# Parameter loads on ScalarE's queue, an activation load ahead of the C matrices, and a negated sine table on VectorE, in a fused S5 + SwiGLU kernel

## The chip, the cores and the metric

The kernel runs on one core of a Trainium2 chip. The metric is the device time of one execution in microseconds, taken as the median over several runs. Beside the runs there is one profiled execution, whose trace is what the views below are read from. All times inside the trace count from the first instruction of the span.

## What is computed

The input `x` (2048 rows of 512 numbers, bf16) is normalised row by row, and three terms are added: the input itself, a state-space layer (S5) and a gated feed-forward layer, both fed by the normalised rows.

```python
xn = layernorm(x)
# S5: diagonal complex recurrence over the 2048 rows
dt      = exp(log_dt);  Lam_bar = exp(dt * (Lambda_re + 1j*Lambda_im))
B_bar   = ((Lam_bar - 1) / Lam)[:, None] * (B_re + 1j*B_im)
Bu      = xn @ B_bar.T
h[t]    = Lam_bar * h[t-1] + Bu[t]
ya      = 2 * (h @ (C_re + 1j*C_im).T).real + xn * Dskip
# SwiGLU, 1376 hidden columns
yb      = (silu(xn @ w_gate) * (xn @ w_up)) @ w_down
out     = x + ya + yb
```

## The kernel before, in words

**Tiling.** The 2048 rows are handled in four chunks of 512 rows (16 tiles of 128 rows). The tile `x_sb` holds all of x, `xn_sb` normalised rows, `xnT` (two buffers, chunk number modulo 2) their transpose, which TensorE (PE) multiplies with the weights. For each chunk PE computes the gate columns (`wg`, line 742) and the up columns (`wu`, line 742) in groups of two 128-column tiles, the leftover columns of two chunks at once (`ffn_left`, lines 820 and 830), the product with B (`BT`, line 857), and at the end the down projection (`wd` with `hT`, line 940, called dA below) and the product with C (`W12` with `hss`, line 953, called dB). dA and dB add up in the same PSUM bank.

**PSUM.** The eight banks are used as four pairs in turn. A group of PE writes a pair, ScalarE (ACT) reads it out (silu into `sg` at line 754, gate; copy into `uf` at line 810, up; copy into `u_sb` at line 864, B; lines 839 to 844, leftover), and only then may the fourth group after it write the same pair.

**Recurrence.** Turning the complex recurrence by a running phase makes it real: VectorE (DVE) multiplies with a cosine table `cosT` and a sine table `sin2` (both tables hold 512 steps for each of four groups of 128 states), scans (line 897), and multiplies back (line 888). `sin2` holds the sine and, beside it, the negated sine. The tables are made in `_tables`: ACT forms the angle (`tm`, line 689), DVE reduces it to one period (lines 691, 693 for sine, 699, 701 for cosine, `scrC`), and ACT applies Sin (lines 695, 697, 703). The small per-state numbers (`sm`, lines 613 to 663, 634, 632) come from three parameter vectors that are loaded as rows of `prow` and transposed by PE (line 565) into `praw`.

**Layer norm.** Chunk 0 is normalised tile by tile in halves at the start, so that PE can begin early (lines 509 to 530 on DVE, `sd` at line 521 on ACT, transposes by PE at line 568). Chunks 1 to 3 take statistics on DVE (lines 479, 483), variance plus epsilon and the power on GpSimd (POOL, lines 487, 491). Chunk 1 is then normalised by DVE (line 495); chunks 2 and 3 by ACT (line 503) after DVE has made `nmr`, minus mean over deviation (line 500). The transpose of chunks 1 to 3 into `xnT` is a DMA transpose (`xt_chunk_dma`, named xTd1 to xTd3 here).

**Order.** Every step is a task of a graph. PE and SyncE (SP) execute their tasks in the order in which the program adds them. For ACT, DVE and POOL `_schedule` chooses the order when the program is built: it keeps a clock per engine from the `est` of each task and, for a DMA, from a byte count, and picks by longest remaining path. So an `est` that is altered costs nothing itself but can reorder ACT and DVE. Each DMA waits in SP's own queue for what it depends on; a DMA transpose waits for every DMA that was added before it, and every later DMA waits for the last transpose:

```python
if xpose:
    after = after + tuple(dma_tasks)
...
else:
    if xp_state[0] is not None:
        after = after + (xp_state[0],)
```

So from `x4` on the loads go one after the other in program order: B_re, B_im (transposes), xTd1, C_re, C_im (transposes), then `ld_x8` (rows of chunk 2), `ld_wd0`, `ld_wd1`, `ld_x12`, `ld_dsk`, then xTd2. On ACT's queue three DMAs stand before any arithmetic: `ld_touch`, a read of 64 short pieces of the gate weights into a tile `tch` that nothing uses, and two parts of the gate weights, `a0` and `a1` (the third, `a2`, is on SP).

Of the kernel before, what the change touches and what calls it, by code (L numbers as in the profile page):

```python
# [10 lines left out]
ALU = alu_op_type.AluOpType  # L11
F32 = mybir.dt.float32
B16 = mybir.dt.bfloat16
I32 = mybir.dt.int32
AF = mybir.ActivationFunctionType

_DBG = {}
_CFG = dict(
    ln_norm_act=(False, False, True, True),
    prio_tab=0.0,  # L20
    prio_par=0.0,
    prio_xt=4000.0,
)
MAGIC = 12582912.0
TWO_PI = 2.0 * math.pi
# [224 lines left out]
def bass_parallel_sum__ssm_conv_s5__swiglu_ffn__prompt_kernel(  # L250
# [23 lines left out]
    KT = D // 128  # L274
# [6 lines left out]
    g = _Graph()  # L281
    es = ExitStack()
    with es:
        block = es.enter_context(nc.Block(no_gpsimd_drain=True))

        def sb(name, shape, dt):
            return es.enter_context(nc.sbuf_tensor(name, shape, dt))
# [7 lines left out]
        x_sb = sb("x_sb", [128, NT, D], B16)  # L295
# [11 lines left out]
        sin2 = sb("sin2", [128, PT, 2, TP], B16)  # L307
# [11 lines left out]
        tz = scrC[:, 2048:3072].rearrange("p (b t) -> p b t", b=2)  # L319
# [4 lines left out]
        mv = sb("mv", [128, NT, 2], F32)  # L324
        ve = sb("ve", [128, NT], F32)
        rstd = sb("rstd", [128, NT], F32)
        nmr = sb("nmr", [128, NT], F32)
        mhalf = sb("mhalf", [128, NT], F32)
        st0 = sb("st0", [128, 4, 2, 6], F32)
        sd0 = sb("sd0", [128, 4], F32)  # L330
        epst = sb("epst", [128, 1], F32)
        tch = sb("tch", [16, KT, 2], B16)
        praw = sb("praw", [128, 3, PT], B16)
        prow = sb("prow", [12, 128], B16)
        ecst = sb("ecst", [128, PT], F32)
# [1 line left out]
        NSM = 64  # L337
        sm = sb("sm", [128, NSM, PT], F32)
# [44 lines left out]
        x_v = A_x[0].rearrange("(a p) d -> p a d", p=128)  # L383
        out_v = out[0].rearrange("(a p) d -> p a d", p=128)
        wg_v = B_w_gate.rearrange("(k p) f -> p k f", p=128)
# [5 lines left out]
        def dma(name, dst, src, writes, nbytes, reads=(), after=(), out_=False, eng="sp", xpose=False, prio=0.0, order=(), **kw):  # L391
            after = tuple(after)
            if xpose:
                after = after + tuple(dma_tasks)
                fn = lambda e, dst=dst, src=src: e.dma_start_transpose(out=dst, in_=src)
                est, nb = 2000.0, int(nbytes * 1.2)
            else:
                if xp_state[0] is not None:
                    after = after + (xp_state[0],)
                fn = lambda e, dst=dst, src=src: e.dma_start(dst, src, **kw)  # L400
                est, nb = 330.0 + nbytes / 900.0, nbytes
            t = g.add(eng, fn, reads=reads, writes=writes, name=name, dma=True, after=after, out=out_, est=est, nbytes=nb, prio=prio, order=order)
            dma_tasks.append(t)
            if xpose:
                xp_state[0] = t
            return t

        TILEB = 128 * D * 2
# [4 lines left out]
        def pload(name, slot, src, **kw):  # L413
            return dma(name, prow[4 * slot:4 * slot + 4, :], src.rearrange("(a p) -> a p", p=128), [("prow", slot)], 1024, **kw)

        def x_load(a, **kw):
            return dma("ld_x%d" % a, x_sb[:, a:a + 1, :], x_v[:, a:a + 1, :], [("x", a)], TILEB, **kw)

        def wg_load(nm, k0, k1, **kw):
            return dma("ld_wg" + nm, wg[:, k0:k1, 0:FG], wg_v[:, k0:k1, 0:FG], [("wg", nm)], (k1 - k0) * 128 * FG * 2, **kw)  # L420

        x_load(0)
        x_load(1)
        act_q = [dma("ld_touch", tch[0:16], wg_v[0:128:8, :, 0:2], [("tch",)], 16 * 16, eng="act")]
        act_q.append(wg_load("a0", 0, 2, eng="act", order=(act_q[-1],)))
        x_load(2)
        act_q.append(wg_load("a1", 2, 3, eng="act", order=(act_q[-1],)))
        wg_load("a2", 3, 4)
        x_load(3)
        pload("ld_ldt", 2, A_log_dt)  # L430
        pload("ld_lim", 1, A_Lambda_im)
        pload("ld_lre", 0, A_Lambda_re)
        dma("ld_wu0", wu[:, :, 0:FH0], wu_v[:, :, 0:FH0], [("wu", 0)], 512 * FH0 * 2)
        dma("ld_wg1", wg[:, :, FG:Fh], wg_v[:, :, FG:Fh], [("wg", 1)], 512 * (Fh - FG) * 2)
# [5 lines left out]
            dma("ld_bim", BT[:, 1], A_B_im, [("BT", 1, kt) for kt in range(KT)], 512 * 512 * 2, xpose=True)  # L440

        def loads_stage_b2():
            dma("ld_cre", CT[:, 0], A_C_re, [("CT", 0)], 512 * 512 * 2, xpose=True)
            dma("ld_cim", CT[:, 1], A_C_im, [("CT", 1)], 512 * 512 * 2, xpose=True)
            dma("ld_x8", x_sb[:, 8:12, :], x_v[:, 8:12, :], [("x", a) for a in range(8, 12)], 4 * TILEB)
            dma("ld_wd0", wd[:, 0:FT - 1, :], B_w_down[0:(FT - 1) * 128, :].rearrange("(k p) d -> p k d", p=128), [("wd", 0)], (FT - 1) * 128 * 1024)
            dma("ld_wd1", wd[0:fsz[-1], FT - 1, :], B_w_down[(FT - 1) * 128:Fh, :], [("wd", 1)], fsz[-1] * 1024)
            dma("ld_x12", x_sb[:, 12:16, :], x_v[:, 12:16, :], [("x", a) for a in range(12, 16)], 4 * TILEB)
            dma("ld_dsk", dsk[:], A_Dskip.partition_broadcast(128), [("dsk",)], 128 * 1024)
# [6 lines left out]
              reads=[("ones",)], writes=[("ident",)], name="ident", est=300)  # L456
        g.add("pool", lambda e: e.iota(iot[:], pattern=[[1, TP]], base=0, channel_multiplier=0, allow_small_or_imprecise_dtypes=True),
              writes=[("iot",)], name="iota", est=1000)
# [1 line left out]
        g.add("pool", lambda e: e.memset(car[:, 0], 0.0), writes=[("car", 0, 0), ("car", 0, 1)], name="car0", est=100)  # L460
        g.add("pool", lambda e: e.memset(ecst[:], math.e), writes=[("ecst",)], name="ecst", est=100)
        def act_table(func, order):
            g.add("act", lambda e: e.activation(out=sm[:, NSM - 1, 0:1], in_=epst[:], func=func, bias=epst[:, 0:1]), reads=[("epst",)], writes=[("sm", "_warm")],
                  name="act_warm", est=1500, order=order)

        act_table(AF.Sqrt, (act_q[-1],))
# [18 lines left out]

        def ln_ve(a, n, eng="dve", order=()):
            return g.add(eng, lambda e: e.tensor_scalar(out=ve[:, a:a + n], in0=mv[:, a:a + n, 1], scalar1=EPS, scalar2=None, op0=ALU.add),
                         reads=[("mv", a + j) for j in range(n)], writes=[("ve", a + j) for j in range(n)], name="ve%d" % a, est=70 if eng == "dve" else 230, order=order)

        def ln_rstd(a, n):  # L490
            return g.add("pool", lambda e: e.tensor_tensor(out=rstd[:, a:a + n], in0=ve[:, a:a + n], in1=mhalf[:, a:a + n], op=ALU.pow),
                         reads=[("ve", a + j) for j in range(n)] + [("mhalf",)], writes=[("rstd", a + j) for j in range(n)], name="rstd%d" % a, est=370 + 190 * n)

        def ln_apply(a, order=()):
            return g.add("dve", lambda e: e.tensor_scalar(out=xn_sb[:, a % NXN, :], in0=x_sb[:, a, :], scalar1=mv[:, a, 0:1], scalar2=rstd[:, a:a + 1],
# [103 lines left out]
        def S(name):  # L599
            if name not in SMI:  # L600
                SMI[name] = len(SMI)
                assert len(SMI) <= NSM
            return sm[:, SMI[name], :]
# [81 lines left out]
        def _tables():  # L685
            thn = S("thn")
            for pt in range(PT):
                b = pt % 2
                g.add("act", lambda e, pt=pt, b=b: e.activation(out=tm[:, b, :], in_=iot[:], func=AF.Identity, scale=thn[:, pt:pt + 1]),
                      reads=R("thn") + [("iot",)], writes=[("tm", b)], name="tm%d" % pt, est=620, prio=_CFG['prio_tab'], order=(hold["evac"],))  # L690
                g.add("dve", lambda e, b=b: e.tensor_scalar(out=tt1[:, b, :], in0=tm[:, b, :], scalar1=MAGIC, scalar2=None, op0=ALU.add),
                      reads=[("tm", b)], writes=[("tt1", b)], name="tt1s%d" % pt, est=400, prio=_CFG['prio_tab'])
                g.add("dve", lambda e, b=b: e.scalar_tensor_tensor(out=tz[:, b, :], in0=tt1[:, b, :], scalar=MAGIC, in1=tm[:, b, :], op0=ALU.subtract, op1=ALU.subtract),
                      reads=[("tt1", b), ("tm", b)], writes=[("tz", b)], name="tzs%d" % pt, est=660, prio=_CFG['prio_tab'])
                g.add("act", lambda e, pt=pt, b=b: e.activation(out=sin2[:, pt, 0, :], in_=tz[:, b, :], func=AF.Sin, scale=-TWO_PI),
                      reads=[("tz", b)], writes=[("sinT", pt, 0)], name="sinT%d" % pt, est=620, prio=_CFG['prio_tab'])
                g.add("act", lambda e, pt=pt, b=b: e.activation(out=sin2[:, pt, 1, :], in_=tz[:, b, :], func=AF.Sin, scale=TWO_PI),
                      reads=[("tz", b)], writes=[("sinT", pt, 1)], name="msinT%d" % pt, est=620, prio=_CFG['prio_tab'])
                g.add("dve", lambda e, b=b: e.tensor_scalar(out=tt1[:, b, :], in0=tm[:, b, :], scalar1=0.25, scalar2=MAGIC, op0=ALU.add, op1=ALU.add),
                      reads=[("tm", b)], writes=[("tt1", b)], name="tt1c%d" % pt, est=400, prio=_CFG['prio_tab'])  # L700
                g.add("dve", lambda e, b=b: e.scalar_tensor_tensor(out=tz[:, b, :], in0=tt1[:, b, :], scalar=MAGIC, in1=tm[:, b, :], op0=ALU.subtract, op1=ALU.subtract),
                      reads=[("tt1", b), ("tm", b)], writes=[("tz", b)], name="tzc%d" % pt, est=660, prio=_CFG['prio_tab'])
                g.add("act", lambda e, pt=pt, b=b: e.activation(out=cosT[:, pt, :], in_=tz[:, b, :], func=AF.Sin, scale=-TWO_PI, bias=halfpi[:, 0:1]),  # L703
                      reads=[("tz", b), ("halfpi",)], writes=[("cosT", pt)], name="cosT%d" % pt, est=700, prio=_CFG['prio_tab'])
# [367 lines left out]
```

## Time and profile before

| | us |
|---|---|
| median of 6 runs | 180.72 (179.88 to 181.54) |
| the profiled execution | 181.39 |
| its span, first to last instruction | 179.6 |
| PE busy in the span | 174.1 (97%) |
| DVE busy | 162.3 (90%) |
| ACT busy | 88.9 (49%) |
| POOL busy | 9.8 (5%) |

The time of the profiled execution holds 1.79 us that lie around the span. Matmuls are pipelined, so a row of PE shows as busy also while one matmul waits for the one in front of it; an idle PE is the surer sign. "Idle before" names what an engine waited for; a wait for several things is put down to the one that came last. The granted TensorE clock is 1.000 for the whole span.

### The profile page before, as it was taken

The numbers are of one execution on the slowest core, as the hardware profiler recorded it, in microseconds if no ns is written. First come the engines' busy times: TensorE is split into PE (matmuls) and PEld (weight loads), VectorE is DVE, ScalarE is ACT, GpSimd is POOL, SyncE is SP. The second block draws the span as 40 slices with busy tenths as digits, with TensorE's granted clock in tenths as the row PEclk, the third lists the DMA queues.
The fourth block names the chain that finished last, engine by engine and source line by source line (L and its number), as shares of the span: only waits on it lengthen the run. The fifth ranks groups of instructions, "written<-read, shape, count | busy, mean of one in ns | idle before, by whom it ended". The sixth has DMA issues, their size and how long they took to land.

```text
span 179.6 us, 2421 instructions
## 1 busy us (share of the span) xinstructions
PE 174.1 (97%) x929; PEld 83.9 (47%) x937; DVE 162.3 (90%) x281; ACT 88.9 (49%) x114; POOL 9.8 (5%) x21
## 2 busy tenths in 40 slices
PE   8899999999979999999999999999999999999994
PEld 2694444444424444444444444444444444444743
DVE  2958984886799999999999999999999999999983
ACT  4469999999499976106656552000965620000000
POOL 3013300000500000040000000000000000000000
DMA  5995585569551000002340000001100000000122
GB/s 166 376 323 96 111 88 95 111 130 362 174 98 22 0 0 0 0 0 65 83 91 0 0 0 4 0 0 58 58 0 4 0 0 0 0 0 4 58 83 92
DMA packets 22978, 12.37 MB, mean 69 GB/s; under 512 B 15192, under 2 KB 22968, under 8 KB 22968
## 3 DMA queue, kind: packets, MB, share of 16 engines
q1 hardware_dynamic: 22472, 11.54, 25.2%
q10 hardware_dynamic: 496, 0.69, 1.1%
q8 instruction: 7, 0.11, 0.3%
q14 instruction: 3, 0.02, 0.1%
HBM read 6.46 MB, written 2.10 MB: 48 GB/s over the span
## 4 chain that ended last, share of the span: by engine, by line
PE 93%; DMA 2%; ACT 2%; DVE 1%; issue 0%; SPq 0%; ACTq 0%
PE pb L742 34%; PE pb L940 21%; PE pb L857 15%; PE pb L953 15%; PE pb L783 3%; DMA x_sb<-in_A_x_dram 2%; PE pb L820 2%; ACT xn_sb L503 1%; PE pb L830 1%; PE pb L568 1%; ACT uf L810 1%; SPq L400 0%; DVE st L509 0%; DVE xn_sb L514 0%; DVE x_sb L958 0%
## 5 line engine op out<-in xcount | busy, mean ns | idle before, releaser
L897 DVE TENSOR_TENSOR_SCAN rot<-sm,car,rot 128x512 bf16<-128x512 f32 x32 | 39.0, 1267 | 0.1
L742 PE MATMUL pb<-xnT,wu 128*128 128x512 bf16 x160 | 37.3, 379 | 1.3 <-ACT uf L810 1.3
L940 PE MATMUL pb<-wd,hT 128*128 128x512 bf16 (+3 forms) x194 | 38.1, 355 | 0.2
L742 PE MATMUL pb<-xnT,wg 128*128 128x512 bf16 x132 | 31.3, 379 | 0.0
L953 PE MATMUL pb<-W,hss 128*128 128x512 bf16 (+2 forms) x140 | 28.1, 355 | 0.2
L857 PE MATMUL pb<-xnT,BT 128*128 128x512 bf16 x128 | 28.1, 379 | 0.0
L940 PEld LDWEIGHTS pb<-wd,hT 128*128 128x128 bf16 (+1 forms) x198 | 18.5, 98 | 19.9
L742 PEld LDWEIGHTS pb<-xnT,wu 128*128 128x128 bf16 x160 | 15.6, 98 | 20.4 <-ACT uf L810 1.8
L754 ACT ACTIVATE sg<-pb 128x1024 bf16<-128x1024 f32 x20 | 20.1, 1025 | 8.4 <-PE pb L742 7.3
L810 ACT ACTIVATE uf<-pb 128x1024 bf16<-128x1024 f32 x20 | 20.6, 1028 | 6.9 <-PE pb L742 6.7
L953 PEld LDWEIGHTS pb<-W,hss 128*128 128x128 bf16 x144 | 13.5, 98 | 14.3
L742 PEld LDWEIGHTS pb<-xnT,wg 128*128 128x128 bf16 x132 | 12.7, 98 | 15.7 <-issue 0.8
L857 PEld LDWEIGHTS pb<-xnT,BT 128*128 128x128 bf16 x128 | 12.5, 98 | 15.1
L864 ACT ACTIVATE u_sb<-pb 128x1024 bf16<-128x1024 f32 x16 | 16.4, 1027 | 4.4 <-PE pb L857 4.1
L812 DVE TENSOR_TENSOR hT<-sg,uf 128x1024 bf16<-128x1024 bf16 x20 | 13.5, 682 | 0.6 <-ACT uf L810 0.6
L888 DVE TENSOR_TENSOR rot<-u_sb,cosT 128x2048 bf16<-128x2048 bf16 x8 | 9.8, 1219 | 2.9 <-ACT cosT L703 2.9
L958 DVE TENSOR_TENSOR x_sb<-pb,x_sb 128x512 bf16<-128x512 f32 (+2 forms) x18 | 10.8, 622 | 1.4 <-PE pb L953 1.4
L503 ACT ACTIVATE xn_sb<-x_sb,nmr,rstd 128x512 bf16<-128x512 bf16 x8 | 5.9, 802 | 10.9 <-DVE nmr L500 10.9
L839 ACT ACTIVATE sg<-pb 96x1024 bf16<-96x1024 f32 x2 | 2.0, 1020 | 17.3 <-PE pb L820 17.3
L479 DVE BATCH_NORM_STATS2 st<-x_sb 128x6 f32<-128x512 bf16 x12 | 7.4, 681 | 2.9 <-DMA x_sb<-in_A_x_dram 2.9
L888 DVE TENSOR_TENSOR rot<-rot,cosT 128x2048 bf16<-128x2048 bf16 x8 | 9.7, 1216 | 0.1
L888 DVE TENSOR_TENSOR rot<-u_sb,sin 128x2048 bf16<-128x2048 bf16 x8 | 9.7, 1218 | 0.0
(78 smaller groups left out, 145.3 us busy)
## 6 DMA issues: line engine op xcount, KB each, us to landing
out_dram<-x_sb SPq DMA_DIRECT2D x15, 128.0 KB, 1.7
x_sb<-in_A_x_dram SPq DMA_DIRECT2D x3, 512.0 KB, 7.7
wd<-in_B_w_down_dram SPq DMA_DIRECT2D x1, 1280.0 KB, 7.2
wu<-in_B_w_up_dram SPq DMA_DIRECT2D x1, 768.0 KB, 5.4
wu<-in_B_w_up_dram SPq DMA_DIRECT2D x1, 608.0 KB, 7.6
x_sb<-in_A_x_dram SPq DMA_DIRECT2D x4, 128.0 KB, 3.5
wg<-in_B_w_gate_dram SPq DMA_DIRECT2D x1, 480.0 KB, 6.5
wg<-in_B_w_gate_dram ACTq DMA_DIRECT2D x1, 448.0 KB, 3.9
```

What stands on the lines that cost most here:

```text
L503: g.add("act", lambda e, a=a: e.activation(out=xn_sb[:, a % NXN, :], in_=x_sb[:, a, :], func=AF.Identity, scale=rstd[:, a:a + 1], bias=nmr ...
L742: inst = e.matmul(pbank[0:fs, bk, :].rearrange("p (j t) -> p j t", j=4), lhsT=w[:, kt, i * 128:i * 128 + fs], rhs=xnT[:, c % 2, :, kt, :], ...
L754: g.add("act", lambda e: e.activation(out=sg[rows, sl, 0:n, :].rearrange("p a t -> p (a t)"), in_=pair_f32(rows, bk, 512 * n), func=AF.Sil ...
L810: g.add("act", lambda e: e.activation(out=uf[rows, ul, 0:n, :].rearrange("p a t -> p (a t)"), in_=pair_f32(rows, bk, 512 * n), func=AF.Ide ...
L812: g.add("dve", lambda e: e.tensor_tensor(out=hT[rows, hb, i0:i0 + n, :], in0=sg[rows, sl, 0:n, :], in1=uf[rows, ul, 0:n, :], op=ALU.mult), ...
L857: inst = e.matmul(pbank[:, bk, :].rearrange("p (j t) -> p j t", j=4), lhsT=BT[:, ri, kt, pt * 128:(pt + 1) * 128], rhs=xnT[:, c % 2, :, kt ...
L864: g.add("act", lambda e: e.activation(out=u_sb[:, us].rearrange("p r t -> p (r t)"), in_=pair_f32(slice(0, 128), b0), func=AF.Identity), r ...
L888: tt = lambda out, a, b, op, r, w, nm: g.add("dve", lambda e: e.tensor_tensor(out=out, in0=a, in1=b, op=op), reads=r, writes=w, name="%s_% ...
L897: g.add("dve", lambda e, A0=A0, A1=A1, k=k, ri=ri, pt=pt: e.tensor_tensor_scan(out=A1[:, k, ri, :], data0=rr[:, pt:pt + 1].to_broadcast([1 ...
L940: inst = e.matmul(pbank[:, bk, 0:nc_], lhsT=hT[0:fs, hb, i, lt * 128:(lt + 1) * 128], rhs=wd[0:fs, i, c0:c0 + nc_], start=(i == 0), stop=F ...
L953: inst = e.matmul(pbank[:, bk, 0:nc_], lhsT=hss[:, hb, pt, ri, lt * 128:(lt + 1) * 128], rhs=W12[:, ri, pt, c0:c0 + nc_], start=False, sto ...
L958: g.add("dve", lambda e, bk=bk, a=a, c0=c0, nc_=nc_: e.tensor_tensor(out=x_sb[:, a, c0:c0 + nc_], in0=pbank[:, bk, 0:nc_], in1=x_sb[:, a, ...
```

## The change

1. On ACT's queue the touch read goes, and two parameter loads (`ld_ldt`, `ld_lim`, 1 KB each) that were on SP take its place ahead of the gate weights.
2. `ld_x8` is added ahead of C_re and C_im.
3. The negated sine is no longer a second Sin on ACT but minus one times the sine, on DVE.
4. Estimates for the scheduler are altered: DMA transposes, `ve` on POOL, `rstd` on POOL.
5. The activation that loads a function table early takes the default bias.

```diff
-        tch = sb("tch", [16, KT, 2], B16)
@@ dma
-                est, nb = 2000.0, int(nbytes * 1.2)
+                est, nb = 1900.0, int(nbytes * 1.2) + 140000
@@ start
-        act_q = [dma("ld_touch", tch[0:16], wg_v[0:128:8, :, 0:2], [("tch",)], 16 * 16, eng="act")]
+        act_q = [pload("ld_ldt", 2, A_log_dt, eng="act")]
+        act_q.append(pload("ld_lim", 1, A_Lambda_im, eng="act", order=(act_q[-1],)))
         act_q.append(wg_load("a0", 0, 2, eng="act", order=(act_q[-1],)))
 ...
-        pload("ld_ldt", 2, A_log_dt)
-        pload("ld_lim", 1, A_Lambda_im)
         pload("ld_lre", 0, A_Lambda_re)
@@ loads_stage_b2
+            dma("ld_x8", x_sb[:, 8:12, :], x_v[:, 8:12, :], ...)
             dma("ld_cre", CT[:, 0], A_C_re, [("CT", 0)], 512 * 512 * 2, xpose=True)
             dma("ld_cim", CT[:, 1], A_C_im, [("CT", 1)], 512 * 512 * 2, xpose=True)
-            dma("ld_x8", x_sb[:, 8:12, :], x_v[:, 8:12, :], ...)
@@ act_table
-            ... e.activation(out=sm[:, NSM - 1, 0:1], in_=epst[:], func=func, bias=epst[:, 0:1]) ...
+            ... e.activation(out=sm[:, NSM - 1, 0:1], in_=epst[:], func=func) ...
@@ ln_ve, on POOL
-  ... est=70 if eng == "dve" else 230 ...
+  ... est=70 if eng == "dve" else 600 ...
@@ ln_rstd
-  ... est=370 + 190 * n)
+  ... est=1000 + 215 * n)
@@ _tables
-  g.add("act", ... e.activation(out=sin2[:, pt, 1, :], in_=tz[:, b, :], func=AF.Sin, scale=TWO_PI),
-        reads=[("tz", b)], ... name="msinT%d" % pt, est=620, ...)
+  g.add("dve", ... e.tensor_scalar(out=sin2[:, pt, 1, :], in0=sin2[:, pt, 0, :], scalar1=-1.0, scalar2=None, op0=ALU.mult),
+        reads=[("sinT", pt, 0)], ... name="msinT%d" % pt, est=200, ...)
```

The built programs differ in this way. PE and POOL execute the same instructions in the same order. SP loses the two parameter loads and has `ld_x8` ahead of the two C transposes. ACT has four Sin fewer; of the rest, the first cosine tables stand earlier among the readouts of B, and the first two of the four normalisations of chunk 2 (line 503) stand ahead of the leftover readout (line 839), the other two behind the first silu of chunk 1; before, all four stood in one block behind that silu. DVE has the statistics of chunk 2 (line 479) right behind the first two products of line 888, ahead of the tables of the second half; before, they stood behind the first scan.

More of the change, by code (lines that the diff above doesn't have):

```diff
@@ L442, in loads_stage_b2 @@
         def loads_stage_b2():
+            dma("ld_x8", x_sb[:, 8:12, :], x_v[:, 8:12, :], [("x", a) for a in range(8, 12)], 4 * TILEB)
             dma("ld_cre", CT[:, 0], A_C_re, [("CT", 0)], 512 * 512 * 2, xpose=True)
             dma("ld_cim", CT[:, 1], A_C_im, [("CT", 1)], 512 * 512 * 2, xpose=True)
-            dma("ld_x8", x_sb[:, 8:12, :], x_v[:, 8:12, :], [("x", a) for a in range(8, 12)], 4 * TILEB)
             dma("ld_wd0", wd[:, 0:FT - 1, :], B_w_down[0:(FT - 1) * 128, :].rearrange("(k p) d -> p k d", p=128), [("wd", 0)], (FT - 1) * 128 * 1024)
@@ L462, in act_table @@
         def act_table(func, order):
-            g.add("act", lambda e: e.activation(out=sm[:, NSM - 1, 0:1], in_=epst[:], func=func, bias=epst[:, 0:1]), reads=[("epst",)], writes=[("sm", "_warm")],
+            g.add("act", lambda e: e.activation(out=sm[:, NSM - 1, 0:1], in_=epst[:], func=func), reads=[("epst",)], writes=[("sm", "_warm")],
                   name="act_warm", est=1500, order=order)
@@ L487, in ln_ve @@
             return g.add(eng, lambda e: e.tensor_scalar(out=ve[:, a:a + n], in0=mv[:, a:a + n, 1], scalar1=EPS, scalar2=None, op0=ALU.add),
-                         reads=[("mv", a + j) for j in range(n)], writes=[("ve", a + j) for j in range(n)], name="ve%d" % a, est=70 if eng == "dve" else 230, order=order)
+                         reads=[("mv", a + j) for j in range(n)], writes=[("ve", a + j) for j in range(n)], name="ve%d" % a, est=70 if eng == "dve" else 600, order=order)
         def ln_rstd(a, n):
             return g.add("pool", lambda e: e.tensor_tensor(out=rstd[:, a:a + n], in0=ve[:, a:a + n], in1=mhalf[:, a:a + n], op=ALU.pow),
-                         reads=[("ve", a + j) for j in range(n)] + [("mhalf",)], writes=[("rstd", a + j) for j in range(n)], name="rstd%d" % a, est=370 + 190 * n)
+                         reads=[("ve", a + j) for j in range(n)] + [("mhalf",)], writes=[("rstd", a + j) for j in range(n)], name="rstd%d" % a, est=1000 + 215 * n)
         def ln_apply(a, order=()):
@@ L696, in _tables @@
                       reads=[("tz", b)], writes=[("sinT", pt, 0)], name="sinT%d" % pt, est=620, prio=_CFG['prio_tab'])
-                g.add("act", lambda e, pt=pt, b=b: e.activation(out=sin2[:, pt, 1, :], in_=tz[:, b, :], func=AF.Sin, scale=TWO_PI),
-                      reads=[("tz", b)], writes=[("sinT", pt, 1)], name="msinT%d" % pt, est=620, prio=_CFG['prio_tab'])
+                g.add("dve", lambda e, pt=pt: e.tensor_scalar(out=sin2[:, pt, 1, :], in0=sin2[:, pt, 0, :], scalar1=-1.0, scalar2=None, op0=ALU.mult),
+                      reads=[("sinT", pt, 0)], writes=[("sinT", pt, 1)], name="msinT%d" % pt, est=200, prio=_CFG['prio_tab'])
                 g.add("dve", lambda e, b=b: e.tensor_scalar(out=tt1[:, b, :], in0=tm[:, b, :], scalar1=0.25, scalar2=MAGIC, op0=ALU.add, op1=ALU.add),
```

## The prediction

> **What bounds the kernel now.** I read the windows first, then the chain that ended last, then the time order around the one hole that they show. The windows have stretches of time, and behind each engine its busy time and its number of instructions.
>
> ```profile
> 7.20:13.70 6.50, 6.50 (x112) 6.32 (x113) 4.43 (x21) 3.97 (x9) 0.88 (x2) 1.00 0.97 329
> 13.70:50.20 36.50, 36.50 (x173) 16.15 (x170) 28.89 (x74) 31.77 (x42) 5.57 (x6) 1.00 0.66 144
> 50.20:51.50 1.30, 0.01 (x1) 0.00 (x0) 1.26 (x2) 1.30 (x3) 0.00 (x0) 1.00 0.00 0
> 51.50:177.30 125.80, 125.33 (x614) 58.74 (x622) 123.94 (x174) 48.98 (x57) 1.90 (x2) 1.00 0.09 24
> ```
>
> PE works without a break from 13.7 to 177.3 us, except from 50.2 to 51.5, where it does nothing while ACT is full. A step elsewhere can only shorten the run by closing this hole or by bringing the start forward. The chain says what filled the hole:
>
> ```profile
> 41.48 7.03 PE pb L742 x32
> 48.50 0.03 ACTq L244
> 48.53 2.03 ACT xn_sb L503 x3
> 50.56 0.92 ACT uf L810
> 51.48 0.05 issue
> 51.52 8.81 PE pb L742 x40
> ```
>
> PE's third up group needed a PSUM pair, whose readout (`uf`, line 810) stood on ACT behind four normalisations (line 503) of chunk 2. The time order gives the reason that these were late:
>
> ```profile
> 38.27 0.37 SPq L400 DMA_DIRECT2D x_sb<-in_A_x_dram  x1
> 41.93 2.47 DVE L479 BATCH_NORM_STATS2 st<-x_sb 128x6 f32<-128x512 bf16 x4 [2.36 <-DMA x_sb<-in_A_x_dram]
> ...
> 47.38 0.16 DVE L500 SCALAR_TENSOR_TENSOR nmr<-mv,rstd 128x4 f32<-128x4 f32 x1 [0.93 <-POOL rstd L491]
> ...
> 47.63 2.93 ACT L503 ACTIVATE xn_sb<-x_sb,nmr,rstd 128x512 bf16<-128x512 bf16 x4 [2.68 <-DVE nmr L500]
> ```
>
> x8 is issued at 38.27, behind both C transposes; DVE waits 2.36 for it; statistics, POOL's two steps and `nmr` follow, and ACT stands idle for 2.68. The load's place is the root.
>
> **x8 ahead of C.** C_re is issued at 29.16, when xTd1 has landed. x8 takes that place. From issue to first use it took 41.93 - 38.27 = 3.66 us, so it is there at 32.8, 9.1 us earlier. DVE has to be free by then: line 479 now stands behind two products of line 888. They began at 31.83 after a wait of 2.85 for the cosine tables, and a product starts every 1.14, so DVE is free at 34.1 at the latest, and at about 32.4 by the table account below. From statistics to `nmr` it was 47.38 - 41.93 = 5.45, so `nmr` is ready at 32.8 + 5.45 = 38.3 (39.6 with DVE late). The table steps that now stand between statistics and `nmr` (two of line 691, two of line 693, one of line 699: 0.85 + 1.2 + 0.4 = 2.4) run while POOL works, which took 47.38 - 44.77 = 2.6.
>
> **ACT behind it.** ACT starts its work from then on at the start-to-start times of the trace: line 503 0.71, line 864 0.92, line 839 1.04, line 841 1.11, line 844 1.24 for two, line 754 0.91. From `nmr` at 38.3 and the 0.25 that ACT took to start: first normalisation 38.55, last readout of B 39.3, second normalisation 40.2, line 839 40.9, line 841 41.9 to 43.0, line 844 to 44.3, silu to 45.3, the two other normalisations to 46.6, then `uf` of the first up group until 47.6. The PSUM pairs are wanted by PE's fourth-next groups at 44.93 (freed 43.0), 46.66 (44.3), 48.39 (45.3) and 50.1 (47.6). The smallest cover is 1.9 us, so `nmr` may be ready as late as 40.2 before PE waits at all. The hole of 1.31 goes whole.
>
> One rule speaks against this. POOL's power now runs beside f32 table steps of DVE; the same power on 128x4 took 1.04, 1.85 and 1.33 us for the three chunks, and 1.85 was the case that the 5.45 above holds. The Trainium skill, "SBUF — State Buffer", on the shared port pair, says that VectorE in a two-port mode and GpSimd exclude each other for a whole instruction. If each of POOL's two steps were locked out for one more DVE step (line 691, 0.42), `nmr` would come 0.84 later, at 39.1 instead of 38.3, and the sum would be the same, since 1.9 is spare. No run here shows whether that lock is what made 1.04 into 1.85.
>
> **What moves behind x8.** The two C transposes come 3.7 later: C_im was through at 38.27 and now is at 42.0. ACT reads C first at 57.63: cover 15. The `wd` loads, x12 and the Dskip row follow from 42.0 instead of 38.7. DMAs of that batch ended by about 48.0 (Dskip issued at 40.48, landed 7.5 later), so now by 51.7 at most. xTd2 waits for all of them: 51.7 instead of 50.62, lands 4.3 to 5.5 later (the spread of the transposes of `xnT`) at 57.2 at most; PE wants it at 60.17 - 1.31 = 58.9. Cover 1.7. `wd` is wanted at 66.0, the Dskip row by DVE (line 592) at about 52, where 0.5 could be lost on DVE alone.
>
> **Negated sine.** Four Sin of 0.62 leave ACT. Four steps on DVE come in. The trace has no such step; line 495, bf16 to bf16 on 128x512, is nearest: 412 ns, started every 0.32; bounds are the 0.17 of a 128x4 step and the 0.42 of line 691. I take 0.32, so 1.3 in all. With two Sin less in front, both first cosine tables are ready when DVE gets to its first product at about 30.1 instead of 31.83. DVE's wait of 2.85 goes, paid partly by two negations (0.64) and by the parameter steps that moved behind chunk 1's statistics (lines 654, 613, 663: 0.95, formerly in the shadow of x4's arrival, which still costs DVE a wait). Those put the first `hT` product from 18.05 to 19.0; ACT's third `uf` needs it at 19.88, still covered.
>
> **What is late next.** dB of the last chunk needs `hss` from DVE:
>
> ```profile
> 167.40 2.35 DVE L888 TENSOR_TENSOR hss<-rot 128x2048 bf16<-128x2048 bf16 x2
> ```
>
> This ends at 169.75 and PE's first dB of that chunk starts at 170.33, so DVE has 0.58 to spare and must gain 0.73 to follow. Up to the first product of the second half of chunk 0 it gains 1.7 (table wait) and most of 2.36 + 0.93 (x8, POOL), less 0.64 for two more negations: over 3 us. Later it cannot run ahead of PE's output, but at its last wait of that kind in the old order (line 846 at 130.56, ACT through at 129.4) it was 1.2 behind; at best it stands there 1.31 + 1.2 = 2.5 earlier. That is three times what it needs.
>
> **The start.** The touch read took ACT 0.44 to issue; the two parameter loads took SP 0.41 and 0.30, so ACT's gate weights go out 0.27 later. `a0` landed at 1.23 + 3.9 = 5.13, now 5.40, wanted at 5.91 with another 0.34 idle behind it; `a1` landed at 6.4, now 6.7, wanted at 7.4. Both covered. The table load moves from 2.23 to 2.50, its end with the small activation from 3.82 to 4.09, where `sd` starts (4.09): 0.03 on the path. The chain goes through x2's arrival at 6.15 with nothing to spare; less traffic ahead of it could give up to 0.1, a full ACT shift would cost 0.27. I take +0.03. SP's later loads go out 0.7 earlier, but the DMA engines are 97% busy from 7.2 to 13.7, so I count nothing. The default bias and the new estimates cost nothing themselves; their orders are in the above.
>
> **Sum.** 181.39 - 1.31 + 0.03 = 180.1 for the profiled execution, span 178.3. That execution lies 0.67 above the median of the runs, so the median goes from 180.72 to 179.4.
>
> **Rivals.**
> - *The touch read had a use* (no change). If the first long load of a queue has to pay what the touch paid (2.2 us to land) in series, `a0` lands at 7.6 against 6.25 that PE can bear: 1.35 lost, 1.31 won, 180.8. For it: the touch stands in front of the weights. Against: a first load of 128 KB took only 2.3 on SP, and a parameter load is a first load as well.
> - *DVE becomes the end's bound, or part of the hole comes back* (no change to slightly faster). If DVE gained nothing, PE could gain 0.5: 180.2. The same if `nmr` comes at 41.0. Against: the covers of 2.5 and 1.9.
> - *x8 lands slowly* (slower). The loads of x took between 2.3 and 8.3 us to land, x4 the longest, in a crowd. Place: the head of SP's serial chain. Each us beyond 3.66 + 1.9 = 5.6 puts PE's wait at line 742 back; from 6.9 on the change loses, from 7.8 by over 0.5%. At 8.3 `nmr` comes at 42.9, PE waits 2.7, and the time is 180.72 - 1.31 + 2.7 + 0.03 = 182.1. Against: at 29.16 no other transfer is under way, and 3.66 was with `wd` right behind.
>
> **Numbers.** 0.5% (0.9 us) is about what a measurement of this kernel can tell from no change. Forecast 0.62 (nearly all of it faster by more than 0.9, a little within), touch 0.12, DVE or a part of the hole 0.10, slow x8 or a like loss in the serial loads 0.16. That makes faster 0.60, same 0.24, slower 0.16. The range goes from 178.5 (start 0.1 better, and half of the runs' own spread of 1.7) to 181.2, which takes in the first two rivals with 0.4 of spread and leaves out the third.
>
> **What would show it.** Right: no idle PE between 13.7 and the end; line 479 of chunk 2 near 32.8; `nmr` near 38.3; L503 split in two pairs on ACT; first cosine product near 30; `hss` of the last chunk done over 1 us before dB. Wrong: PE idle at line 742 between 44 and 52, at line 857 near 59 (xTd2), at line 953 near 169 (`hss`), or first gate matmuls later than 5.9, or 13.7 moved by more than 0.3.

## The result, and the profile after

The changed kernel takes 179.82 us (median of 22 runs, 179.78 to 180.31). The kernel before, over all the comparisons of this study, takes 180.74 (48 runs, 179.88 to 181.67). By the medians that is 0.92 us or 0.5% less. The ratio given with the comparison, 0.9956 with a 95% interval of 0.9945 to 0.9968, makes it 0.8 us, between 0.6 and 1.0. The forecast was 179.4, the range 178.5 to 181.2. Medians below are of executions whose mean granted clock was 0.999 or 1.0; four others, at 0.991, are left out.

The profiled execution of the changed kernel took 179.78 with a span of 178.1. Line numbers of the changed kernel are 1 to 2 lower than before (740 was 742, 477 was 479, 498 was 500, 501 was 503, 808 was 810, 886 was 888, 394 was 395, 399 was 400). The windows, with the same columns as in the prediction:

```profile
13.70:50.20 36.50, 36.50 (x174) 16.36 (x173) 34.21 (x89) 33.18 (x45) 4.94 (x6) 1.00 0.65 144
50.20:51.50 1.30, 1.30 (x8) 0.59 (x7) 1.30 (x3) 1.30 (x3) 0.00 (x0) 1.00 0.00 0
```

In the stretch from 50.2 to 51.5 PE went from nothing to full. DVE's busy time between 13.7 and 50.2 went up by 5.3 and ACT's by 1.4: both engines do work there that they formerly did later, or not at all. The chain that ended last (start, length, what) shows the same without a break:

```profile
13.63 11.22 PE pb L740 x52
24.85 13.81 PE pb L855 x64
38.66 1.73 PE pb L818 x8
40.39 0.98 PE pb L828 x8
41.37 17.37 PE pb L740 x80
```

Before, the last of these five pieces was broken in two, of 7.03 and 8.81, with normalisations and a readout between them; now its 80 matmuls run in one piece of 17.37. From this chain comes a measure that is used throughout below. The third up group of chunk 1 begins 8.81 before the end of the 80, so it stands 41.37 + 17.37 - 8.81 - 13.63 = 36.30 behind the start of the block. In any other execution, the start of that group less the start of its own block less 36.30 is **the hole**. For the profiled execution of before it is 51.52 - 13.73 - 36.30 = 1.49. (The idle time of 1.31 in its row is smaller, since the end of a matmul is modelled and covers a part of the wait.)

The time order around x8, in the changed kernel (start, busy time, engine, line, what, idle time before):

```profile
29.29 0.37 SPq L399 DMA_DIRECT2D x_sb<-in_A_x_dram  x1
32.92 2.47 DVE L477 BATCH_NORM_STATS2 st<-x_sb 128x6 f32<-128x512 bf16 x4 [0.76 <-DMA x_sb<-in_A_x_dram]
37.92 0.16 DVE L498 SCALAR_TENSOR_TENSOR nmr<-mv,rstd 128x4 f32<-128x4 f32 x1
38.39 0.80 ACT L501 ACTIVATE xn_sb<-x_sb,nmr,rstd 128x512 bf16<-128x512 bf16 x1
40.00 0.81 ACT L501 ACTIVATE xn_sb<-x_sb,nmr,rstd 128x512 bf16<-128x512 bf16 x1
44.95 1.51 ACT L501 ACTIVATE xn_sb<-x_sb,nmr,rstd 128x512 bf16<-128x512 bf16 x2
```

x8 is issued 9 us earlier, DVE waits 0.76 for it, and the four normalisations no longer stand in one block of 2.93 in front of the readouts.

### The profile page after: what moved, and what is told of

Same layout as the page of the kernel before. It is cut to its first block, busy times and chain, and to the rows that moved or that the text cites. A ratio compares the mean times of both kernels' runs of the same rounds, so it can differ in the third digit from the quotient of the medians.

```text
span 178.1 us, 2420 instructions
## 1 busy us (share of the span) xinstructions
PE 173.9 (98%) x929; PEld 83.9 (47%) x937; DVE 162.6 (91%) x285; ACT 86.4 (48%) x110; POOL 8.9 (5%) x21
## 4 chain that ended last, share of the span: by engine, by line
PE 94%; DVE 1%; ACT 1%; ACTq 1%; issue 0%
PE pb L740 36%; PE pb L938 21%; PE pb L855 16%; PE pb L951 15%; PE pb L781 3%; PE pb L818 2%; PE pb L828 1%; ACTq L399 1%; ACT L461 1%; PE pb L566 1%; DVE xn_sb L512 1%; DVE st L507 0%; ACT sd L519 0%; DVE rstd L528 0%; DVE x_sb L956 0%
```

## What the hole is worth in other runs

The profiled execution of before took 181.39, which is 0.65 above the median of all 48 runs. The theory formed on seeing the result: **the hole is not one number.** x8 stood at the end of a serial chain of loads and transposes; each run puts it at another time, and PE's wait follows. The profiled execution happened to have one of the largest. Two further profiled executions of the kernel before, with no change in it:

> The kernel before, looked at again. The changed kernel's runs lie within 179.78 to 180.31, those of before within 179.88 to 181.67, and the profiled run of before (181.39) was one of its slowest. Theory H (the hole at PE's line 742 near 50 us has another size in each run): this profile has an idle PE there of another size than 1.31, and its time is about 179.9 plus the true size of the hole (1.48 in the first profile). Rival S (the start varies): the hole is the same, and the first PE group of line 742 starts at another time than 13.73.

> The kernel before, a third look. As for the second: theory H expects hole and time to move together, at a start that stays within 0.15 us of 13.73; rival S expects the start to move and the hole to stay.

The first took 180.43:

```profile
37.35 0.37 SPq L400 DMA_DIRECT2D x_sb<-in_A_x_dram  x1
46.70 2.93 ACT L503 ACTIVATE xn_sb<-x_sb,nmr,rstd 128x512 bf16<-128x512 bf16 x4 [1.65 <-DVE nmr L500]
50.59 1.90 PE L742 MATMUL pb<-xnT,wu 128*128 128x512 bf16 x8 [0.27 <-ACT uf L810]
```

The second took 180.71:

```profile
37.80 0.37 SPq L400 DMA_DIRECT2D x_sb<-in_A_x_dram  x1
46.97 2.93 ACT L503 ACTIVATE xn_sb<-x_sb,nmr,rstd 128x512 bf16<-128x512 bf16 x4 [1.88 <-DVE nmr L500]
50.86 1.90 PE L742 MATMUL pb<-xnT,wu 128*128 128x512 bf16 x8 [0.51 <-ACT uf L810]
```

The same chain is in all three profiles, with x8 at 37.35, 37.80 and 38.27. The start does not explain the times: the block began later in the two shorter executions (13.84 and 13.87, against 13.73). The two experiments below that leave x8 behind the C matrices and keep this wait (`f_start`, `v_ms`) belong in the same table:

| execution | x8 issued | line 503 begins | third up group begins | block begins | hole | time | time less hole |
|---|---|---|---|---|---|---|---|
| before, second profile | 37.35 | 46.70 | 50.59 | 13.84 | 0.45 | 180.43 | 179.98 |
| before, third profile | 37.80 | 46.97 | 50.86 | 13.87 | 0.69 | 180.71 | 180.02 |
| `f_start` | 38.00 | 47.26 | 51.15 | 14.01 | 0.84 | 181.01 | 180.17 |
| before, first profile | 38.27 | 47.63 | 51.52 | 13.73 | 1.49 | 181.39 | 179.90 |
| `v_ms` | 38.13 | 48.18 | 52.08 | 13.80 | 1.98 | 181.91 | 179.93 |

PE's group begins 3.89 or 3.90 behind ACT's first normalisation each time (four normalisations and a readout), and the time without the hole stays within 179.9 to 180.0 while the hole goes from 0.45 to 1.98; the one exception, `f_start` with 180.17, has its block 0.2 later than the others. In the three profiles of the kernel before, the mean time less hole is 179.97, so its median of 180.74 holds a hole of about 0.8, not 1.3 or 1.5, and that is nearly the whole gain.

## The parts one by one

In the kernels named `f_`, and in `g_mid` and `g_a1`, the orders of ACT and DVE are written down as they stand in one of the two kernels, so that an edit cannot reorder them; this shifts their line numbers by 15 to 19 (line 742 is 757 or 759 there). In those named `v_` the scheduler plans anew.

**x8 ahead of the C matrices, nothing else**, with the order of before:

```diff
 def loads_stage_b2():
+    dma("ld_x8", ...)
     dma("ld_cre", ...)
     dma("ld_cim", ...)
-    dma("ld_x8", ...)
```

> The kernel before with one edit: the load of x8 ahead of the C matrices; the order on ACT and DVE is held as it was in before. Statistics of chunk 2 then start when DVE gets there, behind the first scan, at about 39.6 instead of 41.9, so the four normalisations end about 2.3 earlier and the hole should go. Theory H: 179.9 us median, runs within some 0.4 us of each other, ratio about 0.9955. Rival S: the spread of 1.5 us stays, and the median falls by the whole 1.48 to about 179.3.

179.96 (179.85 to 180.02, 6 runs), ratio 0.9963 (0.9948 to 0.9977). The hole is gone, and the spread with it: 0.17 in 6 runs, against 1.0 in 17 runs of the kernel before in the same comparison (180.14 to 181.14, median 180.51). DVE still takes the statistics in their old place, so x8 lies ready for some 7 us:

```profile
28.90 0.37 SPq L417 DMA_DIRECT2D x_sb<-in_A_x_dram  x1
39.59 2.44 DVE L496 BATCH_NORM_STATS2 st<-x_sb 128x6 f32<-128x512 bf16 x4
45.27 2.93 ACT L520 ACTIVATE xn_sb<-x_sb,nmr,rstd 128x512 bf16<-128x512 bf16 x4 [0.22 <-DVE nmr L517]
```

In the chain that ended last, the 80 matmuls are in one piece:

```profile
41.58 17.37 PE pb L759 x80
```

The normalisations begin at 45.27. By the table the wait is zero for a start of about 46.3 or less (46.70 less 0.45), so a normalisation block in one piece is harmless if it comes 1 us earlier. The load's place alone does the work that the prediction gave to it; the new order of ACT and DVE is not needed for that.

**The start alone**: the parameter loads in place of the touch, with the order of before.

```diff
-act_q = [dma("ld_touch", ...)]
+act_q = [pload("ld_ldt", 2, A_log_dt, eng="act")]
+act_q.append(pload("ld_lim", 1, A_Lambda_im, eng="act", order=(act_q[-1],)))
...
-pload("ld_ldt", 2, A_log_dt)
-pload("ld_lim", 1, A_Lambda_im)
```

> The kernel before with one edit: two parameter loads in place of the touch read on ACT's queue; the order on ACT and DVE is held as it was in before. Theory H: the hole and the spread stay, the median is 180.6 to 180.8 (0 to 0.1 better by the start). Rival S: the runs come close together and the median falls by 0.5 to 0.9. Third view (the touch had a use): slower by 0.3 or more, first gate matmuls later than 5.9.

180.99 (180.28 to 182.03, 11 runs), ratio 1.0021 (1.0005 to 1.0038): alone, this part costs a little. It is 0.48 above the median of the runs of before in the same comparison (180.51), as much as the third view asked for, and the first gate matmuls began at 6.01. But that sign does not tell the views apart: in six profiles with the touch these matmuls began between 5.91 and 6.22. What the profile shows of the loads:

```profile
5.15 1.89 SPq L416 DMA_DIRECT2D x_sb<-in_A_x_dram  x1
14.92 2.02 SPq L411 DMA_TRANSPOSE BT<-in_A_B_re_dram  x1
```

x4 is issued 0.59 earlier than in the first profile of before, but its issue takes 1.89 instead of 0.53, and the first transpose, which waits for x4, begins at 14.92; the three profiles of before have 13.94, 13.96 and 14.29. The chain that ended last runs in this profile from x4 through DVE and the transposes to x8. Yet x8 goes out at 38.00, within the 37.35 to 38.27 of before, and the hole of 0.84 is about that of the median of before. What sets this profile apart is the block, which began at 14.01, 0.14 to 0.28 later than in those of before. So the extra cost is measured, but its cause is not shown: a later serial chain is one candidate, a later block another. This kernel also lacks the default bias: the small activation ahead of `sd` takes 0.29 here and 0.20 in the changed kernel.

**The change with the touch back**, in the order of the changed kernel:

> The changed kernel with the touch read back on ACT's queue and the two parameter loads back on SP, its order on ACT and DVE held. With the touch read the first loads ended 0.5 to 0.8 us earlier (first B transpose issued at 13.94 to 14.29, against 14.75 and 14.92 with the parameter loads). Theory: behind the moved x8 nothing waits for that, so the median stays at 179.8 to 180.0. Rival (the late end of the first loads costs time in the changed kernel too): 179.3 to 179.5.

179.88 (179.87 to 179.95, 5 runs), ratio 0.9954 (0.9943 to 0.9966); the block begins at 13.74 against 13.63. With x8 moved, the first transpose at 14.75 costs the changed kernel nothing, and the start is worth 0.06 us between the medians. Single profiles scatter by more than that: with the same parameter loads ahead, `f_start` had 14.01 and `v_nox8` 13.70.

**The change with nothing ahead of the gate weights** on ACT's queue (the parameter loads back on SP, no touch):

> The changed kernel with neither the touch read nor the parameter loads ahead of the gate weights on ACT's queue (the parameter loads back on SP), order held. The chain of the changed kernel begins with ACT's four DMA issues (0.79 to 2.61), the table load and the first sd at 4.14; without two of the issues the table load ends about 0.85 earlier and sd waits for DVE's mean and variance at 3.86 instead: 0.2 to 0.25 faster, 179.55 to 179.65. Rival (something must be sent ahead of the long loads): first gate matmuls later than 6.25, 0.5 or more slower.

180.19 (180.06 to 180.97, 12 runs), ratio 0.9977 (0.9965 to 0.999). I had expected a gain, and it is 0.37 slower than the changed kernel, with the block starting at 13.93 instead of 13.63. The chain that ended last runs here from x0 through `sd`, which came 0.19 later. First the start of DVE and ACT in this kernel:

```profile
0.79 0.99 ACTq L416 DMA_DIRECT2D wg<-in_B_w_gate_dram  x2
3.29 0.69 DVE L542 BATCH_NORM_STATS2 st<-x_sb 128x6 f32<-128x512 bf16 x1 [3.29 <-DMA x_sb<-in_A_x_dram]
4.24 0.29 ACT L536 ACTIVATE sd<-mv,epst 128x1 f32<-128x1 f32 x1 [0.93 <-DVE mv L534]
```

and then the same three in the changed kernel:

```profile
1.66 0.95 ACTq L399 DMA_DIRECT2D wg<-in_B_w_gate_dram  x2
2.95 0.69 DVE L525 BATCH_NORM_STATS2 st<-x_sb 128x6 f32<-128x512 bf16 x1 [2.95 <-DMA x_sb<-in_A_x_dram]
4.05 0.28 ACT L519 ACTIVATE sd<-mv,epst 128x1 f32<-128x1 f32 x1
```

The later the 672 KB of gate weights go out on ACT's queue, the earlier x0 (128 KB, first on SP's queue) is there: 3.29 with the weights at 0.79, 3.15 to 3.22 in the six profiles with the touch (1.23 in the first profile of before), 2.81 to 2.95 in three with both parameter loads (1.66); 3.00 and 3.02 in `g_mid` and `g_a1` below, also at 1.66. In the changed kernel x0 is early enough that `sd` stands on ACT itself: its four issues and the table load.

**The negated sine alone**, planned anew:

```diff
-g.add("act", ... activation(out=sin2[:, pt, 1, :], ..., func=AF.Sin, scale=TWO_PI), ...)
+g.add("dve", ... tensor_scalar(out=sin2[:, pt, 1, :], in0=sin2[:, pt, 0, :], scalar1=-1.0, ...), est=200, ...)
```

> The kernel before with one edit: the negated sine by DVE; the scheduler orders anew. x8 comes as late as before, so theory: the hole stays (0.4 to 1.5 in size by run), median within 0.3 of before, with its spread. Rival (DVE's earlier tables are what closed the hole): 179.9 with little spread.

181.12 (180.78 to 181.97, 9 runs), ratio 1.0028 (1.0012 to 1.0043): slower. The profiled execution:

```profile
44.50 1.11 POOL L487 TENSOR_SCALAR ve<-mv 128x4 f32<-128x4 f32 x1 [25.67 <-DVE mv L483]
45.70 1.86 POOL L491 TENSOR_TENSOR rstd<-ve,mhalf 128x4 f32<-128x4 f32 x1
48.18 2.93 ACT L503 ACTIVATE xn_sb<-x_sb,nmr,rstd 128x512 bf16<-128x512 bf16 x4 [3.17 <-DVE nmr L500]
52.08 1.90 PE L742 MATMUL pb<-xnT,wu 128*128 128x512 bf16 x8 [1.79 <-ACT uf L810]
```

Two Sin less in the stretch are worth nothing to ACT, which waits 3.17 anyway, and DVE's earlier tables (first cosine product at 29.57 instead of 31.83) did not close the hole. The planner puts two products of line 888 beside POOL's steps, and POOL takes 1.11 + 1.86 instead of 0.57 + 1.85; ACT begins 0.59 behind the start of `nmr` instead of 0.25, for which the views name no cause; and the hole is 1.98.

**The whole change, but x8 behind the C matrices**, planned anew:

> The changed kernel with the load of x8 back behind the C matrices; the scheduler orders anew and puts the first up readout of chunk 1 ahead of the four normalisations. Rival (the order on ACT closes the hole by itself, without the load): 179.8 to 180.0. Theory that the load's place is what counts: x8 at about 38.9, nmr at about 47.9, the normalisations end at 51, one more group of PE waits for its pair than is covered: 180.2 to 180.8 with a spread of over 0.5.

180.17 (179.89 to 180.41, 8 runs), ratio 0.9971 (0.9958 to 0.9985): between the theory and the rival, just under the range of the theory and with its spread. x8 is issued at 37.48 and yet the hole is small in the profiled execution, one of the faster (179.99). A row of the time order, and one of the chain that ended last:

```profile
45.43 1.01 ACT L808 ACTIVATE uf<-pb 128x1024 bf16<-128x1024 f32 x1
41.45 17.50 PE pb L740 x80
```

17.50 - 17.37 = 0.13. ACT reads the first up group out ahead of the four normalisations here (45.43 ahead of 47.98), so that PE has one pair more before it must wait. The hole had two remedies, the load's place and ACT's order. The load's place alone leaves nothing of it (`f_x8`); the order alone, with the rest of the change, leaves 0.13 in this profile, and its median is 0.35 above that of the changed kernel. The two do not add up.

**How much cover x8 has**: the changed kernel, its orders held, with x8 between C_re and C_im.

> The changed kernel with the x8 load between C_re and C_im, ACT and DVE in the order of the changed kernel. This is the dose that the prediction's cover speaks of: x8 is issued about 4.5 us later (33.8 for 29.29), so nmr comes at about 42.4 for 37.92. Theory (the chain x8, statistics, POOL, nmr, ACT, PSUM pair, with about 2.5 us of cover in the changed kernel): the last readout of B ends at 44.4, PE waits 1.35 at its first up group (43.05) and 0.5 more at the second, 1.9 in all, and the time is about 181.7. Rival (the order of ACT and DVE alone closes the hole and the load's place hardly matters): 179.8 to 180.1. Rival (the cover is used up and the chain passes on in full, as the smallest cover of the prediction, 1.9, has it): nmr 2.2 behind 40.2, 182.0.

181.93 (181.43 to 182.59, 7 runs), ratio 1.0085 (1.0049 to 1.0121): 2.1 above the changed kernel for a load that comes one transpose later. The profiled execution took 184.72, and its loads came late from the start (first transpose at 15.96, x8 at 35.51), so it is read for the order of waits alone:

```profile
42.95 0.63 ACT L710 ACTIVATE sin<-scrC 128x512 bf16<-128x512 f32 x1 [6.61 <-DVE scrC L708]
44.55 2.73 PE L757 MATMUL pb<-xnT,wg 128*128 128x512 bf16 x8 [3.10 <-ACT u_sb L879]
```

Both of my accounts had the wait behind the normalisations; it is in front of them. The number fits them, the mechanism does not. In this order DVE's statistics stand ahead of the tables of the second half (line 708 of this kernel), ACT waits for these with a Sin, and B's readouts `u_sb` stand behind that Sin. An order that is good for an early x8 is worse than the old one for a late x8.

**A try at a better version**: a1 of the gate weights moved from ACT's queue to SP's, between x2 and a2, so that ACT's table load comes earlier.

> A try at a version better than both: the changed kernel with the gate weights a1 moved from ACT's queue to SP's, between x2 and a2; both parameter loads stay on ACT ahead of a0, and the order of ACT and DVE is held. ACT's table load then comes 0.47 earlier (2.2 for 2.65), and sd waits for the statistics of x0 (3.86) and no longer for ACT (4.05). Theory (ACT's issues are what the start's chain stands on in the changed kernel): sd at 3.9, the whole block from 13.63 comes 0.1 to 0.2 earlier, 179.65 to 179.75. Rival (a1 goes out 0.1 later, a2, x3 and all later SP loads 0.47 later, and one of them is late for a gate matmul): PE waits for wg or x at line 781 and the block starts up to 0.3 later, 179.9 to 180.1.

179.80 (179.68 to 180.45, 8 runs), ratio 0.9964 (0.9931 to 0.9998): that of the changed kernel, no gain. `sd` did come 0.09 earlier, at 3.96. In the profiled execution, the slowest of the eight, the gate weights were late instead:

```profile
6.87 0.95 PE L798 MATMUL pb<-xnT,wg 128*128 128x128 bf16 x14 [0.74 <-DMA wg<-in_B_w_gate_dram]
```

No version in this study beats the changed kernel.

## Why the prediction was right, and where its sizes were off

**The root and the remedy: right.** x8 was issued at 29.29 (29.16 in the prediction), its statistics began at 32.92 (32.8), `nmr` came at 37.92 (38.3), the first normalisation at 38.39 (38.55), the two others as a pair behind the first silu. PE has no idle stretch left. `f_x8` shows that this part alone closes the hole. From statistics to `nmr` it took 5.00 and not 5.45, since POOL's power took 1.46 and not the 1.85 of before.

**The size of the hole: the step that failed.** "The hole of 1.31 goes whole" held for the profiled execution, where it was in fact 1.49 by the chain. The last step, "That execution lies 0.67 above the median of the runs, so the median goes from 180.72 to 179.4", took one execution's hole for that of the median. The 0.67 was the hole's own excess: the other two profiles had 0.45 and 0.69, and the table puts the median's hole at about 0.8. With 0.8 in place of 1.31 the same sum gives 180.72 - 0.8 + 0.03 = 179.95; measured was 179.82. The profile had no second execution in it, but the runs did: they spread over 1.7 us, as much as the hole with some to spare, and a hole at the end of a serial chain is a place where such a spread can come from.

**The start: the sign was off, the size small.** +0.03 was predicted; it is about -0.1 (13.63 against 13.74 in `f_touch`, 0.06 between the medians), no more than single profiles scatter. The issues on ACT took more than counted, 0.56 + 0.26 for the two parameter loads, and the gate weights went out 0.43 later, not 0.27. But x0 landed 0.2 earlier, which the sum did not have, and `sd` began at 4.05 instead of 4.09. The default bias, counted as costing nothing, helped in this: the small activation took 0.20 with it (0.30 before), and `f_start`, with the same loads and the old bias, has `sd` at 4.14. The cover of `a0` was thinner than the 5.40 against 5.91 of the prediction: in `v_nox8` it landed at 6.15 and PE's first gate matmuls waited for it until 6.20. The passage on SP's later loads ("so I count nothing") missed that x4 landed later in spite of its earlier issue (statistics of chunk 1 at 14.38 instead of 14.11); in the whole change nothing hangs on that.

**The rivals.** The touch had no use of the kind that the rival meant: the gate matmuls began at 5.85 (5.91 before), and putting it back gained nothing (`f_touch`, 179.88). Why the change of loads costs time without the moved x8 (`f_start`) stays open. DVE did not become the end's bound: the last chunk's `hss` is done 2.9 ahead of dB, where the prediction had "over 1 us".

```profile
163.53 2.35 DVE L886 TENSOR_TENSOR hss<-rot 128x2048 bf16<-128x2048 bf16 x2
```

x8 did not land slowly (32.92 - 29.29 = 3.63, against 3.66 before). How sharp that rival's edge was, `g_mid` shows: a load that comes one transpose later loses what the change won, and more. Its path was another, though: the rival counted the delay from `nmr` on, and the wait came in earlier, through the tables that DVE makes behind the statistics.

**The negated sine** was rightly counted as no gain of its own. Its steps start every 0.20 and not every 0.32, so four cost DVE some 0.8 instead of 1.3, and the first cosine product began at 29.81 ("about 30.1"). What it does to the plan when made alone (+0.4) the prediction had not asked.

**What moved behind x8** stayed covered: C_im was through at 41.83 (42.0), xTd2 was issued at 50.42 (at most 51.7).

Not settled: how the 0.92 divides to the last tenth. `f_x8` is 0.78 below the 48 runs of before and 0.55 below the 17 taken beside it, and the start is worth 0.06 to 0.1; the rest is within the interval.

## What to carry to other kernels

A load that stands at the end of a serial chain of transposes gathers the delays of all of them; here PE's PSUM pairs had come to depend on it, and moving it ahead removed the wait and the spread of the runs together. Before the size of a hole in one profile goes into a forecast for the median, set that execution's time against the spread of the runs: the excess of a slow one may be the hole itself. And an order planned for an early load should be kept with that load; of the parts of this change, two made the kernel slower when made alone.

## What the runs showed of the hardware that was not expected

**POOL and DVE.** The prediction left open whether a port lock makes POOL's power dearer beside DVE. In the changed kernel:

```profile
35.76 0.60 POOL L485 TENSOR_SCALAR ve<-mv 128x4 f32<-128x4 f32 x1 [16.18 <-DVE mv L481]
36.44 1.46 POOL L489 TENSOR_TENSOR rstd<-ve,mhalf 128x4 f32<-128x4 f32 x1
```

The shortest that the two steps took was 0.25 and 1.04 (chunk 1, kernel before). Here the power began at 36.44 while DVE ran two steps of line 691 of the changed kernel (36.23 to 37.51), the first of which ended, by half of that time, at 36.87; 0.43 and 1.04 make 1.47. That fits one wait, for the DVE instruction that is running. `v_nox8` shows that it can be more than one:

```profile
45.20 2.46 POOL L489 TENSOR_TENSOR rstd<-ve,mhalf 128x4 f32<-128x4 f32 x1
45.55 1.22 DVE L886 TENSOR_TENSOR rot<-rot 128x2048 bf16<-128x2048 bf16 x1
```

There the power began while DVE ran a product of line 844 (44.95 to 45.63) and ended at 47.66, 0.89 behind the end of the next product. So the time of POOL's steps goes with what DVE runs beside them. The Trainium skill, "SBUF — State Buffer", "Who interferes with whom", states that a DVE instruction in a two-port mode contends with GpSimd, as does one with two SBUF inputs when the GpSimd instruction reads SBUF, and that whichever issues first gets the shared ports for its whole length. These rows agree with a wait of that kind. No run here isolates it, or tells for how many DVE instructions a step waits.

**Two queues at the start.** The first load on SP's queue landed between 2.81 and 3.29, the later the earlier the long loads on ACT's queue went out. A small DMA ahead of the long ones on the other queue is, at this start, a delay that helps: taking it away cost 0.37 us against the changed kernel and 0.31 against `f_touch`. At `sd` 0.19 and 0.12 of that is seen; the rest is not traced.
